# Attention block with a hand-written order: row maxima partly from sums and differences of keys, transposed on VectorE

## The chip, the core and the metric

The kernel runs on one core of one Trainium2 chip. The metric is the device time in microseconds of one execution; lower is better. Five engines work side by side: TensorE (PE, with its weight loads as PEld), VectorE (DVE), ScalarE (ACT), GpSimd (POOL) and SyncE (SP), which issues almost all DMAs. Matmuls write to PSUM, which has eight banks of 128 partitions by 512 float32 values.

## The reference, cut to what matters

```python
h  = x + A(layernorm(x))        # x is 2048 x 512
h2 = h + B(layernorm(h))

def A(x):                       # 32 heads of 16 columns
    q, k, v = split(x @ wqkv)   # each 32 x 2048 x 16
    p = softmax(q @ k.T * 16 ** -0.5)
    return (p @ v) @ wo

def B(x):                       # 688 = half of 1376 columns
    z = gelu(x @ w_in)
    g = w_sp @ layernorm(z[:, 688:]) + b_sp
    return (z[:, :688] * g) @ w_out
```

The change concerns A alone. B and the projection by `wo` follow behind it and stay as they are.

## The kernel before

All values are float32. Products that must be exact to float32 are written as three matmuls of a high and a low part (`mm3`, lines 78 to 81), and `split` (line 68) makes the two parts.

**Prologue** (lines 176 to 291). `load_x` and `ln_T` normalise 16 blocks of 128 rows and turn them with TensorE transposes. `proj_v` makes V, which stays in SBUF whole, in a tile with 17 columns to a head, the last of them ones, so that the product with V also gives the sum of the weights. `proj_qk` makes Q and K in four blocks of 128 rows; their parts go to `q_scr` and `k_scr` in HBM, and `load_q` and `load_k` fetch them again in the layout of attention: 48 rows for a head (high, low and high part of Q against high, high and low of K), one head in partitions 0 to 47, one in 64 to 111, and a second pair of heads behind them along the free axis. While the later blocks are projected, `ahead` already makes row maxima, one `max_unit` at a time.

**Attention** (lines 335 to 428). The 32 heads form 8 groups of four, the queries 4 blocks of 512, the keys 16 blocks of 128: 512 units `(hg, qb, kb)`, and 32 groups `g` of 16 units. For each unit

- `score` (lines 344 to 352) makes, head by head, the transposed scores of 128 keys against 512 queries in a PSUM tile `s` of one bank (three of them), and ScalarE takes the exponential (line 351). Two further rows of K and Q (rows 48 and 49) subtract the maximum of the query within the matmul; they are ones in K and the negated maximum, in two parts, in Q.
- `weigh` (lines 354 to 362) multiplies the exponentials of the unit before by V: four heads, each in 32 columns of the array and 32 partitions of one PSUM bank `pv`, accumulated over 16 units. Each of these float32 matmuls stands in the trace as two instructions.
- behind the last unit of a group `gather` (line 364) copies `pv` to SBUF on ScalarE and sends it out in eight DMAs; `invert` (line 376) takes the reciprocals of the sums some units later.

The maxima are an exact row maximum over all 2048 keys. `max_unit(m)` (lines 143 to 158) makes the plain scores of 128 queries against 512 keys for two heads, side by side in two halves of the array's rows, in a PSUM tile `m` of two banks (two of them), and VectorE takes the maximum over both at once (line 156). There are 32 units to a group `g`, 1024 in all. Behind the last, `max_rows` (lines 160 to 173) negates and joins them on VectorE, turns them on TensorE, splits them on VectorE and writes them to the Q tile of that group in four DMAs from SP. The maxima run ahead of the scores by 46 units and more (line 414).

What sets the order: the kernel's framework builds the queue of each engine itself. It takes the instructions that are ready by its own estimate, in the order of the program where it can, and adds the semaphores. So the order of scores, maxima and products on the engines is not that of the source.

**After attention** (lines 432 to 560) come `make_h`, `make_z`, `gate` and `finish`. The first two blocks of `make_h` and three of `load_o` lie inside the last units of attention (lines 419 to 426).

## Time and profile before

| what | us |
|---|---|
| median of 3 runs | 2244.03 (2243.89 to 2246.54) |
| the profiled execution, its own time | 2244.85 |
| its span, first to last instruction | 2243.1 |
| first score matmul | 189.5 |
| start of the last copy of `pv` to SBUF | 1741.6 |
| granted TensorE clock, mean | 0.996 |

The profile is of one execution. A row of a group of instructions has the line, the engine, the operation, the tiles (out<-in), the shapes, the count, then the busy time in us and the mean of one in ns, then the idle time in front of them and what ended it. A row of the timeline has the start in us, the time in us, then the engine, the line and the tiles; several like instructions in a row are merged, with their count. A row of stages has the stretch, its length, then for each engine the busy time and the count, the granted TensorE clock, the busy share of the DMA engines and their rate.

### The profile page before, as it was taken

How to read it: one execution, taken by the hardware profiler on the slowest of the kernel's cores; microseconds unless marked ns; L12 is line 12 of the kernel's file. 1: busy time of each engine (PE TensorE's matmuls, PEld its weight loads, DVE VectorE, ACT ScalarE, POOL GpSimd, SP SyncE). 2: the span in 40 equal slices, each digit the busy share in tenths (PEclk: the TensorE clock that was granted, in tenths of full speed). 3: DMA queues.
4: the chain of work that ended last, by engine and by line, in shares of the span. 5: the costliest groups of instructions: out<-in, count | busy, mean ns of one | idle time of the engine just before them, and what ended most of it. 6: DMA issues, size and time to landing. Idle time of an engine off the chain costs nothing.

```text
span 2243.1 us, 30649 instructions
## 1 busy us (share of the span) xinstructions
PE 2182.3 (97%) x11824; PEld 1103.7 (49%) x11824; DVE 1554.9 (69%) x1940; ACT 1227.7 (55%) x2333; POOL 101.0 (5%) x76
## 2 busy tenths in 40 slices
PE   8999999999999999999999999999999999999999
PEld 6764333333333333333333333333332899999997
DVE  8477778888888888888888888888851787322222
ACT  2114566777766777767777677776776333111111
POOL 2000020000000000000000000000000222200000
PEclk9999999999999999999999999999999999999999
DMA  5553121110020020011012001100101333423221
GB/s 166 116 150 77 29 72 42 30 31 12 20 30 11 17 42 13 11 30 22 18 21 30 13 11 32 27 11 11 33 5 37 97 121 115 155 100 104 83 72 35
DMA packets 81610, 115.17 MB, mean 51 GB/s; under 512 B 22872, under 2 KB 44392, under 8 KB 77880
## 3 DMA queue, kind: packets, MB, share of 16 engines
q1 hardware_dynamic: 81432, 113.21, 19.4%
q8 instruction: 93, 1.52, 0.3%
q14 instruction: 53, 0.43, 0.1%
q0 software_dynamic: 32, 0.01, 0.0%
HBM read 76.98 MB, written 35.26 MB: 50 GB/s over the span
## 4 chain that ended last, share of the span: by engine, by line
PE 89%; ACT 5%; DMA 2%; DVE 2%; issue 1%; SPq 0%; POOL 0%; ACTq 0%; POOLq 0%; DVEq 0%
PE pv L359 28%; PE s L348 24%; PE m L154 10%; PE acc L79 5%; PE acc L81 5%; PE acc L80 5%; ACT pt L351 4%; PE g L80 4%; PE g L79 4%; PE g L81 4%; DMA xg<-in_x 1%; DMA kst<-k_scr 1%; PE tp L539 0%; ACT o L367 0%; DMA rc<-r_scr 0%
## 5 line engine op out<-in xcount | busy, mean ns | idle before, releaser
L156 DVE TENSOR_REDUCE mx<-m 128x2 f32<-128x1024 f32 x1024 | 1220.6, 1222 | 254.3 <-PE m L154 232.5
L351 ACT ACTIVATE pt<-s 128x512 f32<-128x512 f32 x2048 | 1065.6, 603 | 463.7 <-PE s L348 431.6
L348 PE MATMUL s<-qst,kst 50*128 50x512 f32 x2048 | 701.7, 469 | 42.0 <-ACT pt L351 29.1
L359 PE MATMUL pv<-pt,V 128*32 128x512 f32 x4096 | 695.2, 605 | 0.3 <-ACT o L367 0.3
L348 PEld LDWEIGHTS s<-qst,kst 50*128 50x128 f32 x2048 | 283.1, 184 | 698.9 <-issue 434.5
L154 PE MATMUL m<-kst,qst 48*128 48x512 f32 x2048 | 413.7, 417 | 5.2 <-DVE mx L156 2.9
L154 PEld LDWEIGHTS m<-kst,qst 48*128 48x128 f32 x2048 | 214.1, 185 | 147.5 <-DVE mx L156 131.4
L359 PEld LDWEIGHTS pv<-pt,V 128*32 128x32 f32 x4096 | 112.0, 108 | 172.8 <-issue 172.2
L79 PE MATMUL g<-z,ws 128*128 128x344 f32 x512 | 165.3, 323 | 0.5 <-ACT z L472 0.5
L80 PE MATMUL g<-z,ws 128*128 128x344 f32 x512 | 164.6, 322 | 0.0
L81 PE MATMUL g<-z,ws 128*128 128x344 f32 x512 | 163.4, 319 | 0.0
L71 ACT ACTIVATE ws<-wt 128x1024 fp32r<-128x1024 f32 x32 | 33.6, 1055 | 211.4 <-PE g L80 203.5
L528 DVE SCALAR_TENSOR_TENSOR pr<-g,bias,z 128x344 f32<-128x344 f32 x32 | 18.4, 576 | 182.2 <-PE g L81 180.1
L80 PEld LDWEIGHTS g<-z,ws 128*128 128x128 f32 x512 | 96.1, 188 | 5.8 <-issue 5.2
L79 PEld LDWEIGHTS g<-z,ws 128*128 128x128 f32 x512 | 96.2, 188 | 0.9 <-ACT z L472 0.8
L81 PEld LDWEIGHTS g<-z,ws 128*128 128x128 f32 x512 | 96.2, 188 | 0.6
L315 POOL TENSOR_TENSOR o<-o,rc 128x512 f32<-128x512 f32 x16 | 20.6, 1290 | 1480.6 <-DMA rc<-r_scr 1263.8
L79 PE MATMUL acc<-wi,hT 128*128 128x344 f32 x256 | 83.1, 325 | 0.0
L80 PE MATMUL acc<-wi,hT 128*128 128x344 f32 x256 | 81.8, 319 | 0.0
L81 PE MATMUL acc<-wi,hT 128*128 128x344 f32 x256 | 81.8, 319 | 0.0
L472 ACT ACTIVATE z<-acc 128x344 f32<-128x344 f32 x64 | 29.2, 458 | 82.8 <-PE acc L81 77.4
L71 ACT ACTIVATE part<-acc 128x512 fp32r<-128x512 f32 x32 | 19.1, 597 | 97.3 <-PE acc L81 83.0
(105 smaller groups left out, 1382.5 us busy)
## 6 DMA issues: line engine op xcount, KB each, us to landing
wt<-in_w_sp SPq DMA_DIRECT2D x16, 1024.0 KB
qst<-q_scr SPq DMA_DIRECT2D x192, 64.0 KB
kst<-k_scr SPq DMA_DIRECT2D x48, 256.0 KB
k_scr<-part SPq DMA_DIRECT2D x16, 512.0 KB
q_scr<-part SPq DMA_DIRECT2D x16, 512.0 KB
z_scr<-z SPq DMA_DIRECT2D x16, 344.0 KB
z<-z_scr SPq DMA_DIRECT2D x16, 344.0 KB
xg<-in_x SPq DMA_DIRECT2D x16, 256.0 KB
```

Of the source, the lines that this page charges most:

```text
L71: nc.scalar.activation(hi, src, AF.Copy)
L79: nc.tensor.matmul(ps, lh, rh, start=first, stop=False)
L80: nc.tensor.matmul(ps, lh, rl, start=False, stop=False)
L81: nc.tensor.matmul(ps, ll, rh, start=False, stop=last)
L154: nc.tensor.matmul(t[:, j, :], q[r, p, u * P:(u + 1) * P], k[r, p, c * 512:(c + 1) * 512], start=True, stop=True)
L156: nc.vector.reduce_max(mx[g][:, :, p * 4 + u, c], t, axis=AX.X)
L315: nc.gpsimd.tensor_mul(o, o, rc)
L348: nc.tensor.matmul(s, k[r, h // 2, kb * P:(kb + 1) * P], q[r, h // 2, :], start=True, stop=True)
L351: nc.scalar.activation(t, s, AF.Exp, scale=DH ** -0.5)
L359: nc.tensor.matmul(pv[0][32 * j:32 * j + 32, :], V[:, kb, c:c + 32], pts[j], start=kb == 0, stop=kb == NB - 1)
L472: nc.scalar.activation(zc_, acc[:, :FC], AF.Gelu_apprx_tanh)
L528: nc.vector.scalar_tensor_tensor(pr[:, f], g[i][:, :FC], bias[:, tb:tb + 1], z1[:, f], op0=ALU.add, op1=ALU.mult)
```

## The change

It has these parts.

1. **Order.** `tc.manual_schedule` makes the queues of PE, ACT and DVE (in the prologue SP too) follow the source. The prologue is written out block by block: V, Q and K, the layer norm of two blocks at a time with its last step on ScalarE, and a `take` of each PSUM result one projection later. In attention one round of the loop is two units, and the eight steps of a `max_pair` stand at fixed places among scores and products.
2. **Scores.** A tile `s` has two banks (two tiles instead of three single banks); two heads go into it side by side, and one exponential takes 1024 values to a partition.
3. **Maxima.** A `max_pair` covers 128 queries, two heads (t = 0, 1) and all keys, in eight matmuls of one bank each (three banks, one buffer each). Head t = 1 takes four maxima over 512 keys. For head t = 0 the kernel also keeps the sum and the difference of keys 0 to 511 and 512 to 1023 (`uv`, made in the prologue, through HBM to a tile `uvs`). Since max(a, b) is half of (a + b) + |a - b|, ScalarE takes the absolute value of the scores against the differences, and one VectorE instruction adds the scores against the sums, halves and takes the maximum; two plain maxima cover the other 1024 keys. So VectorE takes seven operands of 512 where it took four of 1024. Maxima run 11 pairs ahead.
4. **Transpose of the maxima.** The negation stays on VectorE, the split goes to POOL, the turning from TensorE to a VectorE transpose of 32 by 32 blocks one round later, and eight DMAs instead of four write the rows.
5. **Accumulator.** `pv` is taken out in halves, one on VectorE, one on ScalarE, and between the product that ends a group and the one that begins the next the order puts other work.
6. **Data.** V goes through HBM (`v_scr`) and comes back for four heads at a time (`load_v`, a POOL copy puts it into place). The heads of a group are numbered by `head`, the rows of Q and K stand interleaved by three, and `load_uv` adds three DMAs for each group of heads.

```diff
-LEAD = 46
-LEAD0 = 40
+LEAD = 11
 KM = 50
+PB = 6
+FIRST = 3
...
-    ps_m = attn.enter_context(tc.tile_pool(name="ps_m", bufs=2, space=PSUM, side="right"))
-    V = vpool.tile([P, NB, H * VW + DH - 1], F32, name="V")
+    ps_m = attn.enter_context(tc.tile_pool(name="ps_m", bufs=1, space=PSUM, side="right"))
+    VP = NB * 4 * VW
+    vst = [vpool.tile([P, VP + DH], F32, name=f"vst{i}") for i in range(2)]
     kst = [kpool.tile([RG + KM, 2, S], F32R, name="kst0")]
-    qst, mx = {}, {}
+    uvs = [kpool.tile([KS, 2, 1024], F32R, name="uvs0")]
...
+    def head(hg, p, t):
+        return 8 * (hg // 2) + 4 * t + 2 * (hg % 2) + p
     def load_k(hg, pieces=range(6)):
-        r = slice(64 * hg, 64 * hg + 64)
         for j in pieces:
             j, t = divmod(j, 2)
-            r0 = RG * t + 16 * j
+            h0 = DH * head(hg, 0, t)
             nc.sync.dma_start(
-                kst[hg % 2][r0:r0 + 16, :, :].bitcast(F32),
-                k_scr[(0, 0, 1)[j], r, :].rearrange("(p t r) s -> t r p s", t=2, r=DH)[t])
+                kst[hg % 2][RG * t + j:RG * t + KS:3, :, :].bitcast(F32),
+                k_scr[(0, 0, 1)[j], h0:h0 + 2 * DH, :].rearrange("(p r) s -> r p s", r=DH))
+    def load_uv(hg, pieces=range(3)):
+        r = slice(32 * (hg % 2), 32 * (hg % 2) + 32)
+        for j in pieces:
+            nc.sync.dma_start(
+                uvs[hg % 2][j:KS:3, :, :].bitcast(F32),
+                uv_scr[(0, 0, 1)[j], hg // 2, r].rearrange("(p r) i s -> r p (i s)", r=DH))
+    def load_v(hg):
+        raw = vpool.tile([P, NB, 4 * DH], F32, name="raw")
+        for t in range(2):
+            c = DH * head(hg, 0, t)
+            nc.sync.dma_start(raw[:, :, 2 * DH * t:2 * DH * t + 2 * DH],
+                              v_scr[:, c:c + 2 * DH].rearrange("(a p) c -> p a c", p=P))
+        nc.gpsimd.tensor_copy(
+            vst[hg % 2][:, :VP].rearrange("p (a c) -> p a c", c=VW)[:, :, :DH],
+            raw.rearrange("p a (h c) -> p (a h) c", c=DH))
...
-    def max_unit(m):
-        g, i = divmod(m, 32)
+                    qst[g][RG * t + j:RG * t + KS:3, :, :].bitcast(F32),
+                    q_scr[(0, 1, 0)[j], h0:h0 + 2 * DH, c].rearrange("(p r) s -> r p s", r=DH))
+    more = {}
+    def bank(i):
+        if i in more:
+            return more[i]()
+        return ps_m.tile([P, 512], F32, name=f"m{i}")
+    def max_pair(m):
+        g, i = divmod(m, 8)
         hg, qb = divmod(g, NQ)
...
+        q, k, w = qst[g], kst[hg % 2], uvs[hg % 2]
         if i == 0:
...
+            mx[g] = sm.tile([P, 16, 4], F32, name="mx")
+            nc.gpsimd.memset(mx[g][:, :8, 3:], LOW)
+        c, p = slice(i % 4 * P, i % 4 * P + P), i // 4
+        at = lambda t, e: mx[g][:, t * 8 + i, e:e + 1]
+        def scores(t, keys, b):
+            r = slice(RG * t, RG * t + KS)
+            acc = bank(b)
+            nc.tensor.matmul(acc, q[r, p, c], keys[r, p], start=True, stop=True)
+            return acc
+        def one(t, e, b):
+            acc = scores(t, k[:, :, 512 * e:512 * e + 512], b)
+            nc.vector.reduce_max(at(t, e if t else e - 1), acc, axis=AX.X)
+        def minus(b):
+            acc = scores(0, w[:, :, 512:], b)
+            ab[0] = sm.tile([P, 512], F32, name="ab")
+            nc.scalar.activation(ab[0], acc, AF.Abs)
+        def plus(b):
+            acc = scores(0, w[:, :, :512], b)
+            nc.vector.tensor_tensor_reduce(ab[0], acc, ab[0], 0.5, LOW, ALU.add, ALU.max, at(0, 0))
+        def last(b):
+            one(0, 3, b)
+            if i == 7:
+                nm = sm.tile([P, 2, 8], F32, name="nm")
+                nc.vector.tensor_reduce(nm.rearrange("p t i -> p (t i)"), mx.pop(g), axis=AX.X,
+                                        op=ALU.max, negate=True)
+                parts = sm.tile([P, 2, 2, 8], F32R, name="mparts")
+                split(parts[:, :, 0], parts[:, :, 1], nm, "pool", "pool")
+                turned[0] = (g, parts)
+        ab = {}
+        four = [lambda b, e=e: one(1, e, b) for e in range(4)]
+        return [four[0], lambda b: one(0, 2, b), minus, four[1], four[2], four[3], plus, last]
+    def max_rows():
+        g, parts = turned.pop(0)
+        t = sm.tile([P, 32], F32, name="mturned")
+        nc.vector.transpose(t, parts.bitcast(F32).rearrange("p t j i -> p (t j i)"))
+        for n in range(P // 32):
+            for j in range(2):
+                r0 = RG * j + KS
+                nc.sync.dma_start(
+                    qst[g][r0:r0 + 2].bitcast(F32).rearrange("r p (c n s) -> r (p c) n s", n=4, s=32)[:, :, n],
+                    t[32 * n + 16 * j:32 * n + 16 * j + 16, :])
...
+                hh = P // 2
+                if which == 1 and n < 2:
+                    kf[n] = p2.tile([P, 512], F32, name=f"kf{n}", bufs=1)
+                    nc.scalar.activation(kf[n][:hh], acc[:hh], AF.Copy)
+                    nc.scalar.activation(kf[n][hh:], acc[:hh], AF.Copy, scale=1.0 - 2.0 * n)
+                if which == 1 and n == 1:
+                    uv = p2.tile([P, 512], F32, name="uv", tag="xn")
+                    nc.gpsimd.tensor_add(uv, kf[0], kf[1])
+                    part = p2.tile([P, 2, 512], F32R, name="part", bufs=PB)
+                    split(part[:, 0, :], part[:, 1, :], uv, "pool", "pool")
+                    for i in range(2):
+                        nc.sync.dma_start(uv_scr[:, b, :, i, :].rearrange("i p s -> p i s"),
+                                          part[hh * i:hh * i + hh].bitcast(F32))
...
+        todo, done = [], [0]
+        def ahead(k):
+            for _ in range(k):
+                m = done[0] // 8
+                if not todo and m < LEAD:
+                    steps = max_pair(m)
+                    todo.extend(steps[i] for i in (0, 1, 3, 2, 4, 6, 5, 7))
+                if todo:
+                    todo.pop(0)(done[0] % 5)
+                    done[0] += 1
...
+            for j in range(24):
+                b, n, i = 1 + j // 8, j // 2 % 4, 1 - j % 2
+                def between(d):
+                    if d == 1 and j >= FIRST:
+                        ahead(5)
+                    if d == 2 and takes:
+                        takes.pop(0)()
+                    if d == 3 and turned and done[0] % 8 > 3:
+                        max_rows()
+                if j in (2, 10):
+                    put = load_wqk(b + 1)
+                if j in (5, 13):
+                    put()
+                if j == 4:
+                    load_v(0)
+                if j in (8, 12):
+                    load_q(j // 4 - 1)
+                if j == 16:
+                    fixed(kst[0])
+                takes.append(proj_qk(b, n, i, between))
+            takes.pop(0)()
+            ahead(8 * LEAD - done[0])
+        m = LEAD
...
-        def score(hg, qb, kb, h):
+        def score(hg, qb, kb, p):
             q, k = qst[hg * NQ + qb], kst[hg % 2]
-            s = ps_s.tile([P, 512], F32, name="s")
-            r = slice(RG * (h % 2), RG * (h % 2) + KM)
-            nc.tensor.matmul(s, k[r, h // 2, kb * P:(kb + 1) * P], q[r, h // 2, :],
-                             start=True, stop=True)
-            t = pp.tile([P, 512], F32, name="pt")
+            s = ps_s.tile([P, 2, 512], F32, name="s")
+            for t in range(2):
+                r = slice(RG * t, RG * t + KM)
+                nc.tensor.matmul(s[:, t, :], k[r, p, kb * P:(kb + 1) * P], q[r, p, :],
+                                 start=True, stop=True)
+            t = pp.tile([P, 2, 512], F32, name="pt")
             nc.scalar.activation(t, s, AF.Exp, scale=DH ** -0.5)
...
-                c = (4 * hg + j) * VW
-                nc.tensor.matmul(pv[0][32 * j:32 * j + 32, :], V[:, kb, c:c + 32],
-                                 pts[j], start=kb == 0, stop=kb == NB - 1)
-            if kb == NB - 1:
-                gather(hg, qb)
-            o = sm.tile([P, 512], F32, name="o", bufs=1)
-            nc.scalar.activation(o, pv[0], AF.Copy)
+            o = pp.tile([P, 512], F32, name="o", bufs=1)
+            nc.vector.tensor_copy(o[:, :256], pv[0][:, :256])
+            nc.scalar.activation(o[:, 256:], pv[0][:, 256:], AF.Copy)
...
-        for n, (hg, qb, kb) in enumerate(units):
-            if hg + 1 < HG and n % 64 < 24 and n % 4 == 1:
-                load_k(hg + 1, [n % 64 // 4])
-            if kb == 1 and n // NB + 3 < HG * NQ:
-                load_q(n // NB + 3)
-            pts = [score(hg, qb, kb, h) for h in range(2)]
-            if prev is not None:
-                weigh(*prev)
-            pts += [score(hg, qb, kb, h) for h in range(2, 4)]
-            prev = (hg, qb, kb, pts)
-            if kb == 5 and n > NB:
-                invert()
-            while m < min(LEAD0 + 9 * (n + 1) // 4, LEAD + 2 * (n + 1), 32 * HG * NQ):
-                max_unit(m)
+        with tc.manual_schedule(engines={E.PE, E.Activation, E.DVE}):
+            for n in range(0, len(units), 2):
+                (hg, qb, kb), (_, _, kb1) = units[n:n + 2]
+                if hg + 1 < HG and n % 64 < 24 and n % 4 == 0:
+                    load_k(hg + 1, [n % 64 // 4])
+                if hg + 1 < HG and n % 64 < 12 and n % 4 == 2:
+                    load_uv(hg + 1, [n % 64 // 4])
+                if hg + 1 < HG and n % 64 == 30:
+                    load_v(hg + 1)
+                if kb == 2 and n // NB + 3 < HG * NQ:
+                    load_q(n // NB + 3)
+                steps = max_pair(m) if m < 8 * HG * NQ else []
                 m += 1
-            if n % 32 == 16 and n < 6 * 32:
-                load_weights(n // 32)
-            if n == 480:
-                load_o(0)
-            if n == 504:
-                make_h(0, ps_m.tile([P, 2, 512], F32, name="m")[:, 0, :])
-                load_o(1)
-            if n == 508:
-                make_h(1, ps_m.tile([P, 2, 512], F32, name="m")[:, 0, :])
-                load_o(2)
-        weigh(*prev)
-        invert()
+                step = lambda b: steps and steps.pop(0)(b)
+                pts = [score(hg, qb, kb, 0), score(hg, qb, kb, 1)]
+                step(2)
+                step(0)
+                if prev is None:
+                    pv[0] = ps_v.tile([P, 512], F32, name="pv")
+                    for j in range(4):
+                        nc.tensor.matmul(pv[0][32 * j:32 * j + 32, :], vst[0][:, :32],
+                                         vst[0][:, :512], start=True, stop=True)
+                else:
+                    weigh(*prev)
+                step(1)
+                if kb == 0 and n:
+                    gather(*units[n - 1][:2])
+                step(2)
+                pts1 = [score(hg, qb, kb1, 0)]
+                step(0)
+                pts1.append(score(hg, qb, kb1, 1))
+                step(1)
+                step(2)
+                weigh(hg, qb, kb, pts)
+                if turned:
+                    max_rows()
+                step(1)
+                prev = (hg, qb, kb1, pts1)
+                if kb == 6 and n > NB:
+                    invert()
+                if n % 32 == 16 and n < 6 * 32:
+                    load_weights(n // 32)
+                if n == 480:
+                    load_o(0)
+                if n == 504:
+                    make_h(0, bank(0))
+                    load_o(1)
+                if n == 508:
+                    make_h(1, bank(0))
+                    load_o(2)
+            weigh(*prev)
+            gather(*prev[:2])
+            invert()
     attn.close()
```

256 lines of the change are left out of this document (148 added, 108 removed).

## The prediction

> **What bounds the kernel now.** I read the page first, then a table of stages, then the steady part of attention instruction by instruction.
>
> ```profile
> span 2243.1 us, 30649 instructions
> ...
> PE 2182.3 (97%) x11824; PEld 1103.7 (49%) x11824; DVE 1554.9 (69%) x1940; ACT 1227.7 (55%) x2333; POOL 101.0 (5%) x76
> ...
> PE 89%; ACT 5%; DMA 2%; DVE 2%; issue 1%; SPq 0%; POOL 0%; ACTq 0%; POOLq 0%; DVEq 0%
> ```
>
> ```profile
> 0.00:189.50 189.50, 177.17 (x743) 124.16 (x743) 130.40 (x286) 36.64 (x61) 18.88 (x22) 0.96 0.54 142
> 189.50:1742.00 1552.50, 1509.71 (x8169) 520.92 (x8169) 1207.23 (x1134) 1082.89 (x2083) 31.06 (x17) 1.00 0.12 25
> 1742.00:2243.00 501.00, 495.37 (x2912) 458.61 (x2912) 217.26 (x521) 108.16 (x190) 51.05 (x37) 1.00 0.30 98
> ```
>
> PE is called busy everywhere, but the end of a matmul is modelled, so the share says little. The stages (prologue, attention, rest) say where to look: attention takes 1552 of 2243 us, and in it neither DVE (1207) nor ACT (1083) is full. So I look at one unit; the timelines of PE, of DVE and of ACT in the same stretch:
>
> ```profile
> 751.26 1.11 PE L359 MATMUL pv<-pt,V 128*32 128x512 f32 x8
> 752.29 0.50 PE L348 MATMUL s<-qst,kst 50*128 50x512 f32 x2
> 752.63 0.65 PE L154 MATMUL m<-kst,qst 48*128 48x512 f32 x4
> 753.11 0.91 PE L348 MATMUL s<-qst,kst 50*128 50x512 f32 x2
> 753.95 1.11 PE L359 MATMUL pv<-pt,V 128*32 128x512 f32 x8
> 755.00 0.50 PE L348 MATMUL s<-qst,kst 50*128 50x512 f32 x2
> ```
>
> ```profile
> 753.06 2.36 DVE L156 TENSOR_REDUCE mx<-m 128x2 f32<-128x1024 f32 x2 [0.35 <-PE m L154]
> ```
>
> ```profile
> 752.88 2.06 ACT L351 ACTIVATE pt<-s 128x512 f32<-128x512 f32 x4 [0.64 <-PE s L348]
> ```
>
> ```profile
> 753.53 0.18 PEld L348 LDWEIGHTS s<-qst,kst 50*128 50x128 f32 x1 [0.47 <-ACT pt L351]
> ```
>
> A unit takes 752.29 to 755.00, 2.71 us. It is a circle: ACT waits 0.64 us for the first score; the fourth score waits for the end of the first exponential, because `s` has three banks; `pv` stands behind the fourth score; the next unit's first score stands behind `pv`. No engine is full; the order and the banks make the 2.71. Between units stands one disturbance in each group of 16:
>
> ```profile
> L163 DVE TENSOR_REDUCE nm<-mx x20: 219/220/222, 663.6 to 1562.5; 128x16 f32<-128x64 f32 x20
> ```
>
> ```profile
> 900.19 1.04 PE L359 MATMUL pv<-pt,V 128*32 128x512 f32 x2
> ...
> 901.17 0.28 PE L166 MATMUL m<-ident,nm 128*16 128x128 f32 x1
> ...
> 901.48 0.28 DVE L75 CAST mpart<-m 16x128 fp32r<-16x128 f32 x1 [1.27 <-PE m L166]
> ...
> 902.03 1.06 PE L359 MATMUL pv<-pt,V 128*32 128x512 f32 x6
> ```
>
> A group takes (1562.5 - 663.6) / 19 = 47.31 us, 16 x 2.71 is 43.4, so `max_rows` costs 3.9: DVE waits for the turning, and the four heads of `pv` fall apart into two and six instructions, each part at the 1.04 us of all eight. Two units cost 47.31 / 8 = 5.91.
>
> **The change part by part.** First the prices, from the groups by shape.
>
> ```profile
> L156 DVE TENSOR_REDUCE mx<-m 128x2 f32<-128x1024 f32 x1024 | 1220.6, 1222 | 254.3 <-PE m L154 232.5 <-PE s L348 20.5
> L351 ACT ACTIVATE pt<-s 128x512 f32<-128x512 f32 x2048 | 1065.6, 603 | 463.7 <-PE s L348 431.6 <-PE m L154 31.6
> ...
> L71 ACT ACTIVATE ws<-wt 128x1024 fp32r<-128x1024 f32 x32 | 33.6, 1055 | 211.4 <-PE g L80 203.5 <-DMA wt<-in_w_sp 7.2 <-PE acc L80 0.7
> ...
> L76 DVE TENSOR_TENSOR part<-acc,part 128x512 fp32r<-128x512 f32 x32 | 21.9, 685 | 14.4 <-ACT part L71 14.3
> ...
> L239 DVE COPY V<-acc 128x512 f32<-128x512 f32 x16 | 11.0, 688 | 7.9 <-PE acc L81 7.8
> ...
> L71 ACT ACTIVATE o<-o 128x512 fp32r<-128x512 f32 x16 | 10.1, 630 | 9.0 <-PE acc L80 5.5 <-issue 2.0 <-POOL o L315 1.5
> ```
>
> ```profile
> 85.02 0.39 PE L80 MATMUL acc<-xT,wqk 128*128 128x512 f32 x1
> 85.24 0.39 PE L81 MATMUL acc<-xT,wqk 128*128 128x512 f32 x1
> ```
>
> *DVE, 512 from PSUM:* 0.69 (copy and two-operand row); two reductions back to back take 2.36, not 2.44, so 0.08 overlaps: 0.61. *ACT:* four exponentials in 2.06, so (2.06 - 0.60) / 3 = 0.49 each; 1024 instead of 512 adds 1.055 - 0.630 = 0.43, so 0.92 each, 1.03 alone. *PE:* a matmul 0.23; the first behind `pv` 0.34 (752.29 to 752.63); the one before `pv` 0.42 (753.53 to 753.95); `pv` itself 1.04; matmuls in the two halves of the rows side by side at no price, as the s x2 and m x4 rows show.
>
> *One round (two units) in the new order, PE.* First half: `last` 0.34, two score pairs 0.23 each, the maxima matmuls `four0` and `one2` side by side 0.42, `pv` 1.04: 2.26. Second half: `minus` with `four1` 0.34, score pair 0.23, `four2` beside one head of the next pair 0.23, its other head 0.23, `four3` with `plus` 0.42, `pv` 1.04: 2.49. Sum 4.75, if nothing waits.
>
> *The waits that the single banks add.* `plus` needs the bank of `four1`: matmul 0.50 (the duration of the first row behind `pv`), about 0.05 to the reader, reduction 0.69, 0.05 back: 1.29 behind the start of the half, where PE alone would be there after 1.03. `four3` needs the bank of `minus`, which ScalarE empties: 0.59 (752.29 to 752.88), 0.60, 0.05: 1.24. So 0.26 more: **5.01 a round** against 5.91. Queued behind these waits on PE are `pv`, `last` and the next scores; on ACT the absolute value stands ahead of the exponentials three and four, which are wanted only a round later.
>
> *Do the others keep up?* ACT: 4 x 0.92 + 0.49 = 4.17, and the next round's second score needs the fourth exponential's bank: the third starts at about 3.3 (behind the absolute value, 2.26 + 0.59 + 0.49), the fourth ends at 3.3 + 0.92 + 1.03 = 5.25, wanted at 5.01 + 0.57. It fits. DVE: 7 x 0.61 = 4.3 to 7 x 0.69 = 4.8, with the work of a group's end (negation 0.22, transpose, half copy and reciprocal, each between that and 0.69, so about 1.1 in eight rounds) 4.4 to 5.0. It just fits. The new instruction that adds, halves and takes the maximum is in no row: from below 0.69 (L76 reads the same two operands), from above 1.22 (as if it read them one after the other, L156). I take 0.69, since L76 is the nearest row.
>
> *Transpose of the maxima:* the 3.9 of each group go. On PE nothing is left of it. The split on POOL has 3 us until the transpose; POOL is busy 31 us in all of attention. SP issues eight DMAs:
>
> ```profile
> 901.79 2.83 SPq L172 DMA_DIRECT2D qst<-mpart  x4
> ```
>
> 8 x 0.71 = 5.7 and the landing, for which I take 2 to 4. From the transpose (late in the round with kb 10) to the first score of the next group are three rounds less 4.6, so 10.4 us. It fits with 1 to 3 us to spare.
>
> *Accumulator in halves:* the product behind it finds its bank empty; ACT's half (between 0.28 and 0.60) pushes exponentials three and four, for which 0.3 is to spare. I allow 0.3 for each of 31 group ends: 9.
>
> *Prologue.* Before, 40 `max_unit`s stand between projection matmuls:
>
> ```profile
> 117.63 0.40 PE L81 MATMUL acc<-xT,wqk 128*128 128x512 f32 x1
> 117.96 0.49 PE L154 MATMUL m<-kst,qst 48*128 48x512 f32 x2
> 118.38 0.50 PE L79 MATMUL acc<-xT,wqk 128*128 128x512 f32 x1
> 118.72 0.39 PE L80 MATMUL acc<-xT,wqk 128*128 128x512 f32 x1
> ```
>
> One costs 1.09 - 2 x 0.23 = 0.63, 40 of them 25. After, 88 matmuls come in 18 batches of five, three slots each: 0.63 + 2 x 0.23 = 1.09, 20 in all. The same 576 projection matmuls stay. So the first score comes at 189.5 - 25 + 20 = 184, if the waits stay as they are. DVE has 0.61 x 4.4 + 0.69 = 3.4 for each projection of 2.7 + 1.1, so it does not hold PE. V through HBM, `uv` and their DMAs hide behind 0.54 DMA share; `load_v(0)` has 19 projections until its use. K has to be there before the first maxima:
>
> ```profile
> 107.21 0.70 PE L154 MATMUL m<-kst,qst 48*128 48x512 f32 x2 [1.18 <-DMA kst<-k_scr]
> ```
>
> Before, PE waited for it; now six projections (16 us) stand between, and SP, whose order is fixed here too, holds V's writes behind `load_k`'s wait, for which the six buffers are cover. Without the cover some 5 us.
>
> *Tail.* From round 245 on no maxima are left: ACT sets the pace, 4 x 0.92 = 3.7, eleven rounds 40. The two `make_h` inside stand in PE's fixed order with 12 matmuls, 3.3 each: 7. ACT and DVE now wait in order for the data of `load_o(0)`: 0 to 10, I take 3.
>
> **The sum.** 184 + 245 x 5.01 (1227) + 9 + 40 + 7 + 3 = 1470 at the last copy of `pv`, where it was 1741.6; the rest, 2243.1 - 1741.6 = 501.5, is untouched: span 1971.5, and the 1.75 us that the execution (2244.85) has beyond its span: **1973**. The profiled execution lies 0.04% above the median of the runs, so nothing is to be scaled.
>
> **The rivals.**
>
> *PE without waits.* If the banks come free in time (shorter matmul-to-reader times than the 0.55), a round is 4.75: 245 x 0.26 = 64 less, 1909. For it: PE is the fullest engine. Against: the 0.50 and the 0.59 are rows.
>
> *VectorE becomes the bound.* Seven reductions of 512 where there were four of 1024: none overlaps its neighbour, since each now waits for its own matmul, and the new instruction costs 1.22: 6 x 0.69 + 1.22 + 0.14 = 5.5 a round, 245 x 0.49 = 120 more, 2093; with half of that, 2033. The Trainium skill speaks for this one: its page "VectorE: DVE Perf Modes", section "Rules for kernel authors", asks for few instructions, as each ends with a flush of the pipeline that a missing semaphore doesn't save. By that rule the count decides, and it goes from four to seven; the trace agrees that 0.16 of the 0.69 is not streaming (1.22 - 0.69 = 0.53 is what 512 more cost).
>
> *The maxima come late.* If a DMA of the rows costs twice 0.71 in queue and landing, 13.4 are needed where 10.4 are to be had: 3 at each of 31 group ends, 93 more, 2066.
>
> *The order does not hold what it says:* the group ends keep their 3.9 (from another wait, such as ACT's or DVE's head of the queue on `load_o`, `sums` or the accumulator): 31 x 3.9 = 121 more, 2094.
>
> *Slower.* The new VectorE instruction streams at a quarter of the pace: 4 x 0.53 + 0.16 = 2.3. DVE then needs 6 x 0.69 + 2.3 + 0.14 = 6.6 a round, 245 x 1.6 = 390 more, 2363. It decides from about 6.1 a round, (1741.6 - 184 - 59) / 245, that is from 1.8 for this instruction, 2.7 times the row of L76. For it speaks only that the trace has no such instruction.
>
> **How the numbers follow.** Forecast 1973: 0.50, from 1940 to 2010 by the bounds of prologue, `load_o` and group ends. PE without waits 0.15, VectorE 0.14, late maxima 0.08, order 0.07, slower 0.04; 0.02 for no change by some of these together. The range goes from 1890 (the first rival with a K that no longer waits) to 2085, which takes in late maxima and most of VectorE's. Faster 0.94, same (within 0.2%, 4.5 us, about what a measurement of this kernel can tell) 0.02, slower 0.04.
>
> **What would show it.** In the profile after: rounds of 5.0 us between the starts of every second `pv`, with `four3`/`plus` waiting about 0.3 for ACT or DVE; groups at 40 us by the `nm` rows; the first score at 184; DVE at nine tenths in attention; the new instruction at 0.69. If DVE is full and PE waits for it in front of `four0`, the VectorE rival holds; if scores wait for DMAs of the `mturned` rows, the maxima are late.

## The result, and the profile after

The changed kernel takes 1943.5 us (median of four runs, 1942.1 to 1945.3), the kernel before 2244.0 in the same session: a ratio of 0.866, with a 95% interval of 0.8645 to 0.8675. Forecast were 1973 us and a range of 1890 to 2085. One run of those below, of the kernel before in a fixed order, came at a lower clock than the other three and 1.9% above the fastest of them; its ratio leaves it out.

The page of the changed kernel, its first lines and the head of its chain of work:

```profile
span 1943.5 us, 32016 instructions
...
PE 1916.7 (99%) x11800; PEld 1096.1 (56%) x11800; DVE 1443.8 (74%) x2916; ACT 1266.8 (65%) x1591; POOL 139.2 (7%) x200
...
PE 92%; DVE 2%; ACT 2%; issue 1%; DMA 1%; SPq 0%; POOL 0%; ACTq 0%; DVEq 0%
```

The table of stages, cut at the first score and at the last copy out of `pv` (span; then busy time of PE, PEld, DVE, ACT and POOL with their counts, granted clock, DMA share, GB/s):

```profile
0.00:184.50 184.50, 170.03 (x745) 125.25 (x745) 118.78 (x283) 59.34 (x98) 36.08 (x49) 0.98 0.69 181
184.50:1441.00 1256.50, 1251.04 (x8144) 512.53 (x8144) 1109.55 (x2112) 1100.01 (x1304) 50.49 (x113) 0.99 0.15 36
1441.00:1943.00 502.00, 495.61 (x2914) 458.28 (x2912) 215.41 (x521) 107.43 (x190) 52.62 (x38) 1.00 0.30 100
```

The prologue is 5 us shorter, attention 296 us shorter, and the rest as long as it was. In the prologue TensorE is busy for 170.0 us where it was 177.2, 7.1 less where 5 less were forecast, and idle for 14.5 where it was 12.3. In attention VectorE now has work for 1110 of 1257 us, ScalarE for 1100.

The groups, by the negation of the maxima that each group has once (the view of one line, in the steady stretch from 700 to 1300 us):

```profile
L217 DVE TENSOR_REDUCE nm<-mx x15: 220/220/221, 718.8 to 1265.3; 128x16 f32<-128x64 f32 x15
```

That is (1265.3 - 718.8) / 14 = 39.04 us a group, or 4.88 a round, where it was 47.31 and 5.91. One round in the timeline of TensorE, and the stretch of VectorE and ScalarE that belongs to its second half:

```profile
800.50 0.50 PE L197 MATMUL m<-kst,qst 48*128 48x512 f32 x1
800.50 0.96 PE L537 MATMUL s<-qst,kst 50*128 50x512 f32 x4
801.24 0.45 PE L197 MATMUL m<-kst,qst 48*128 48x512 f32 x2
801.62 1.07 PE L548 MATMUL pv<-pt,vst 128*32 128x512 f32 x8
802.62 0.49 PE L197 MATMUL m<-uvs,qst 48*128 48x512 f32 x1
802.62 0.50 PE L197 MATMUL m<-kst,qst 48*128 48x512 f32 x1
802.95 0.40 PE L537 MATMUL s<-qst,kst 50*128 50x512 f32 x2
803.20 0.39 PE L197 MATMUL m<-kst,qst 48*128 48x512 f32 x1
803.33 0.50 PE L537 MATMUL s<-qst,kst 50*128 50x512 f32 x2
803.82 0.50 PE L197 MATMUL m<-kst,qst 48*128 48x512 f32 x1
803.93 0.49 PE L197 MATMUL m<-uvs,qst 48*128 48x512 f32 x1
804.35 1.06 PE L548 MATMUL pv<-pt,vst 128*32 128x512 f32 x8
805.34 0.49 PE L197 MATMUL m<-kst,qst 48*128 48x512 f32 x1
```

```profile
803.18 1.89 DVE L202 TENSOR_REDUCE mx<-m 128x1 f32<-128x512 f32 x3 [0.23 <-PE m L197]
804.99 0.68 DVE L211 CUSTOM_DVE_ANT_0 ab<-m,ab 128x512 f32<-128x512 f32 x1
```

```profile
803.16 0.60 ACT L207 ACTIVATE ab<-m 128x512 f32<-128x512 f32 x1
```

The round takes 4.84 us, 800.50 to 805.34; over the 600 us of steady attention the starts of every second `pv` lie 4.87 apart in the median. The first half goes from 800.50 to 802.62, 2.12 us without a wait. The second takes 2.72: behind `minus` and `four1` (802.62) and the scores stands `four3` (803.82), which needs the bank that ScalarE's absolute value left at 803.16 + 0.60, and then `plus` (803.93), which needs the bank of the reduction that began at 803.18. The product `pv` starts only behind them. These are the two waits that the prediction named. Over 600 us of attention they are the two waits for a bank that count; the table of waits (us in total, times, longest; a weight load that waits beside a running matmul is counted too, and 278 waits in 123 rounds are more than those of `plus`, so the sums are larger than what the round loses):

```profile
PEld m L197 <- DVE mx L202: 213.5, 278, 0.8
...
PEld m L197 <- ACT ab L207: 38.6, 123, 0.4
```

One group is not like the others: group 30 begins late, and the copies out of `pv` around its start stand 44.5 us apart instead of 39.0. TensorE and SP's queue there:

```profile
1356.62 0.49 PE L197 MATMUL m<-kst,qst 48*128 48x512 f32 x1
1359.88 1.85 PE L537 MATMUL s<-qst,kst 50*128 50x512 f32 x4 [2.77 <-DMA qst<-mturned]
```

```profile
1343.45 9.71 SPq L497 DMA_DIRECT2D rc<-r_scr  x10
1353.27 6.05 SPq L235 DMA_DIRECT2D qst<-mturned  x8
```

SP's order is left to the planner in attention, and it put the small DMAs of the first `load_o` ahead of the eight DMAs that carry the maxima. The scores waited 2.77 us for those, and the group lost about as much again behind the wait (44.5 - 39.0 - 2.8 = 2.7): the granted clock in the next ten microseconds is 0.50 (last but two of the columns).

```profile
1360.00:1370.00 10.00, 10.00 (x38) 4.13 (x38) 5.31 (x10) 5.58 (x8) 0.00 (x0) 0.50 0.06 12
```

### The profile page after: what moved, and what is told of

Same layout as the page of the kernel before. It is cut to its first block, busy times and chain, and to the rows that moved or that the text cites. A ratio compares the mean times of both kernels' runs of the same rounds, so it can differ in the third digit from the quotient of the medians.

```text
span 1943.5 us, 32016 instructions
## 1 busy us (share of the span) xinstructions
PE 1916.7 (99%) x11800; PEld 1096.1 (56%) x11800; DVE 1443.8 (74%) x2916; ACT 1266.8 (65%) x1591; POOL 139.2 (7%) x200
## 4 chain that ended last, share of the span: by engine, by line
PE 92%; DVE 2%; ACT 2%; issue 1%; DMA 1%; SPq 0%; POOL 0%; ACTq 0%; DVEq 0%
PE pv L548 25%; PE m L197 25%; PE s L537 13%; PE acc L84 6%; PE acc L85 5%; PE acc L86 5%; PE g L85 4%; PE g L84 4%; PE g L86 4%; ACT pt L540 1%; PE tp L754 1%; DMA rc<-r_scr 0%; PE tp L671 0%; DVE rs_t L99 0%; PE tp L197 0%
## 5 line engine op out<-in xcount | busy, mean ns | idle before, releaser
L540 ACT ACTIVATE pt<-s 128x1024 f32<-128x1024 f32 x1024 | 994.1, 1029 | 148.1 <-PE s L537 140.2
L202 DVE TENSOR_REDUCE mx<-m 128x1 f32<-128x512 f32 x1511 | 958.4, 683 | 112.9 <-PE m L197 70.9
L197 PE MATMUL m<-kst,qst 48*128 48x512 f32 x1511 | 609.8, 449 | 0.0
L548 PE MATMUL pv<-pt,vst 128*32 128x512 f32 x4096 | 547.5, 606 | 0.0
L537 PE MATMUL s<-qst,kst 50*128 50x512 f32 x2048 | 472.6, 431 | 6.9 <-DMA qst<-mturned 2.8
L197 PE MATMUL m<-uvs,qst 48*128 48x512 f32 x503 | 250.0, 498 | 0.0
L197 PEld LDWEIGHTS m<-uvs,qst 48*128 48x128 f32 x503 | 92.1, 183 | 208.8 <-DVE mx L202 206.1
L211 DVE CUSTOM_DVE_ANT_0 ab<-m,ab 128x512 f32<-128x512 f32 x252 | 171.2, 679 | 3.7 <-ACT ab L207 2.0
L207 ACT ACTIVATE ab<-m 128x512 f32<-128x512 f32 x251 | 151.0, 602 | 18.6 <-PE tp L197 10.4
L84 PE MATMUL acc<-wi,hT 128*128 128x344 f32 x256 | 83.1, 325 | 0.0
L85 PE MATMUL acc<-wi,hT 128*128 128x344 f32 x256 | 81.8, 319 | 0.0
```

The source lines that it names most:

```text
L84: nc.tensor.matmul(ps, lh, rh, start=first, stop=False)
L85: nc.tensor.matmul(ps, lh, rl, start=False, stop=False)
L197: nc.tensor.matmul(acc, q[r, p, c], keys[r, p], start=True, stop=True)
L202: nc.vector.reduce_max(at(t, e if t else e - 1), acc, axis=AX.X)
L207: nc.scalar.activation(ab[0], acc, AF.Abs)
L211: nc.vector.tensor_tensor_reduce(ab[0], acc, ab[0], 0.5, LOW, ALU.add, ALU.max, at(0, 0))
```

## The experiments

The theory at this point: a round is TensorE's own time plus the wait of `plus` and `four3`, and the fixed order is what keeps the round and frees the group ends of their 3.9 us. That the place of the turn of the maxima decides the group ends became the theory only after the fourth run. Rivals were that VectorE's work sets the round, that the order alone does it, and, later, that it is the turn's engine or the shape of the scores. Each kernel is told by its edit; groups are read as above, from the rows of `nm` between 700 and 1300 us.

**Four plain maxima for each head.** Head t=0 takes its maxima like head t=1, without sums, differences and absolute value:

```diff
-            nc.vector.reduce_max(at(t, e if t else e - 1), acc, axis=AX.X)
+            nc.vector.reduce_max(at(t, e), acc, axis=AX.X)
...
-        return [four[0], lambda b: one(0, 2, b), minus, four[1], four[2], four[3], plus, last]
+        return [four[0], lambda b: one(0, 2, b), lambda b: one(0, 0, b), four[1], four[2],
+                four[3], lambda b: one(0, 1, b), last]
```

> The changed kernel, but head t = 0 takes four plain maxima over 512 keys like head t = 1: no sums and differences in the maxima, no absolute value on ScalarE; order and all else kept. Theory (the round is PE's order plus the wait for the banks of the second half): the bank of the third-last matmul now comes free by a second VectorE reduction, 1.90 us behind the start of the half instead of 1.29, so a round goes from 4.85 to about 5.45, a group of 16 units from 39.0 to about 43.7, the whole to about 2090 us. Rival (VectorE's work alone counts: eight times 0.61 instead of seven): 4.85 to 5.1, about 2000 us. Rival (the order is the whole gain): no change, 1943 us.

Measured 2082.7 us, ratio 0.928 (0.926 to 0.930). The rows of `nm`, and VectorE's timeline in one round:

```profile
L216 DVE TENSOR_REDUCE nm<-mx x13: 220/220/221, 740.3 to 1265.6; 128x16 f32<-128x64 f32 x13
```

```profile
812.92 3.08 DVE L201 TENSOR_REDUCE mx<-m 128x1 f32<-128x512 f32 x5 [0.24 <-PE m L196]
```

Groups take 43.8 us: five reductions follow each other in the second half, 3.08 us, and TensorE waits for them. So the sums and differences are worth 139 us here, 4.7 a group, close to what the theory said: with them, one of the five banks of the second half goes to ScalarE, which reads it beside VectorE.

**Two matmuls less, VectorE's work kept.** `minus` and `plus` are left out with ScalarE's absolute value (so head t=0's maxima are incomplete); VectorE reduces 512 constants in SBUF in the place of `plus`:

```diff
+    still = const.tile([P, 512], F32, name="still")
+    nc.gpsimd.memset(still, LOW)
...
-        return [four[0], lambda b: one(0, 2, b), minus, four[1], four[2], four[3], plus, last]
+        none = lambda b: None
+        kept = lambda b: nc.vector.reduce_max(at(0, 0), still, axis=AX.X)
+        return [four[0], lambda b: one(0, 2, b), none, four[1], four[2], four[3], kept, last]
```

> The changed kernel without the matmuls minus and plus and without the absolute value; VectorE instead takes a maximum over 512 constants in SBUF at the place of plus, so it keeps seven instructions of 512 a round. It leaves out keys 0 to 1023 from the maximum of head t = 0. Theory (the wait for the banks of the second half sets the round, not VectorE's work): no bank is used twice in the second half, the round falls to what PE needs, 2.12 + 2.36 = 4.5 us, a group to about 36, the whole to about 1860 us. Rival (VectorE is the bound): round stays at 4.8 to 4.85, 1940 us.

Measured 1878.2 us, ratio 0.837 (0.836 to 0.838). The rows of `nm`, and the 600 us of steady attention in a table of stages:

```profile
L219 DVE TENSOR_REDUCE nm<-mx x16: 220/220/221, 726.4 to 1283.1; 128x16 f32<-128x64 f32 x16
```

```profile
700.00:1300.00 600.00, 593.04 (x3870) 234.27 (x3870) 575.07 (x968) 504.80 (x532) 13.09 (x52) 1.00 0.13 28
```

Groups of 37.1, 4.64 a round. So the two matmuls, their banks and ScalarE's absolute value, which went out together, carry 65 us of the 1943: the rival's 1940 us is ruled out, and the theory's 1860 us and groups of 36 are missed by 18 us and 1.1 us. With 575 of 600 us VectorE is nearly full here, and in its table of waits those of the maxima matmuls for VectorE are the longest in total for TensorE (242.5 us in 315 waits), so the floor is not TensorE's alone. The VectorE rival was wrong for the changed kernel and becomes right about 5% below it.

**The changed kernel without the fixed order in attention.** The prologue keeps it:

```diff
-        with tc.manual_schedule(engines={E.PE, E.Activation, E.DVE}):
+        with ExitStack():
             for n in range(0, len(units), 2):
```

> The changed kernel with the fixed order taken away in attention alone: PE, ACT and DVE are queued by the framework's planner there; the prologue keeps its order. Theory (the order is needed for the round of 4.85): the four heads of pv fall apart again and the maxima are pulled between the scores, a group takes 43 to 48 us instead of 39.0, the whole 2070 to 2230 us. Rival (the shorter work of VectorE, the wide exponentials and the transpose on VectorE make the gain whatever the order): a group 39 to 40, 1945 to 1975 us.

Measured 2044.5 us, ratio 0.911 (0.909 to 0.912), between the two forecasts: the first is wrong about the steady groups, the rival about the ends. Its rows of `nm`, and two stages, cut at the copies out of `pv` of its first and its fourth group:

```profile
L217 DVE TENSOR_REDUCE nm<-mx x15: 219/220/222, 723.7 to 1270.3; 128x16 f32<-128x64 f32 x15
```

```profile
242.70:428.00 185.30, 176.08 (x778) 62.30 (x777) 109.11 (x206) 109.64 (x127) 27.02 (x22) 0.85 0.18 48
428.00:1420.00 992.00, 990.71 (x6496) 408.64 (x6496) 908.09 (x1725) 874.54 (x1041) 18.26 (x82) 1.00 0.13 30
```

The steady groups take 39.04, as in the fixed order: the planner finds the same round. It loses at the start, where three groups take 185 us in place of 117 with a clock of 0.85, starts attention at 195.1 instead of 184.5, and takes 133 us for the last three groups in place of 120. There the first forecast's mechanism does act: the planner pulls the maxima ahead, and from 241.6 to 281 us TensorE runs 48 maxima matmuls beside 12 of the scores. In attention the fixed order is worth 101 us, and all of it at the ends; in the prologue it was not tried.

**The kernel before in a fixed order.** TensorE, ScalarE and VectorE are held to the source order in its attention:

```diff
-        for n, (hg, qb, kb) in enumerate(units):
+        with tc.manual_schedule(engines={E.PE, E.Activation, E.DVE}):
+            for n, (hg, qb, kb) in enumerate(units):
...
```

> The kernel before, with PE, ACT and DVE held to the order of the source in attention, nothing else: scores of two heads, pv of the unit before, scores of the other two, two maxima. Theory (order alone isn't enough: with three single banks the second score of a unit waits for the third exponential of the unit before, 1.24 + 0.42 + 1.0 us behind each other): 2.66 a unit where it was 2.71, a group 43 to 45 us because the group ends and the ends of attention get shorter, the whole 2100 to 2150 us. Rival (order is the whole gain): a unit 2.4, a group 39 to 40.5, 1970 to 2010 us.

Measured 2274.7 us (median of four, 2262.7 to 2304.7), ratio 1.012 (1.0075 to 1.016): some 26 us slower, and both forecasts missed. TensorE's timeline at a group end, and the stretch behind it:

```profile
884.81 0.27 PE L166 MATMUL m<-ident,nm 128*16 128x128 f32 x1 [2.55 <-DVE nm L163]
```

```profile
886.20:896.40 10.20, 10.20 (x44) 4.55 (x40) 5.11 (x5) 5.53 (x11) 0.00 (x0) 0.51 0.01 3
```

The turn is asked for right behind the last maxima, and in a fixed order TensorE stands before it until VectorE has reduced and negated: 2.55 us. After that the granted clock is halved, here for 10.2 us, and behind the last turn for 68 us. Units at full clock take 2.71 as they did; a group takes 48.05. So the order alone does not shorten this kernel, and with the turn at this place the group ends cost more in a fixed order than under the planner; the place of the turn was next to be tried.

**The changed kernel again,** with no edit, beside the next three kernels on one chip, as the measure for small differences:

> The changed kernel unchanged, on the same chip as the other three, as the measure for differences of a few us: 1942 to 1946 us by every theory.

Measured 1943.2 us, ratio 0.866 (0.864 to 0.867).

**The changed kernel with its maxima turned by TensorE.** The transpose goes back to TensorE and bank 0, with VectorE's split from PSUM and four DMAs, at the changed kernel's place:

```diff
-        t = sm.tile([P, 32], F32, name="mturned")
-        nc.vector.transpose(t, parts.bitcast(F32).rearrange("p t j i -> p (t j i)"))
+        t = bank(0)
+        nc.tensor.transpose(t[:16, :P], nm.rearrange("p t i -> p (t i)"), ident)
+        part = sm.tile([16, 2, P], F32R, name="mpart")
+        split(part[:, 0, :], part[:, 1, :], t[:16, :P])
...
```

> The changed kernel, with one part taken back: the row maxima are turned by TensorE into bank 0 and split by VectorE from PSUM, with four DMAs in place of eight; the order and all else stay as changed. Theory (a turn in TensorE is cheap once its place is fixed and its input is there long before; the 3.9 us of each group were a wait in an order that asked for the maxima too soon): TensorE pays the turn of 0.28 and two changes of kind of matmul, VectorE two small instructions of 0.28 and a wait, together 0.5 to 1.2 us for each of 29 groups in attention: groups 39.5 to 40.2, 1958 to 1978 us. Rival (the turn in TensorE is itself what cost the 3.9): groups 43, 2055 to 2070 us.

Measured 1946.4 us, ratio 0.867 (0.866 to 0.868) against 1943.2 unchanged. Its rows of `nm`, and TensorE behind the product:

```profile
L217 DVE TENSOR_REDUCE nm<-mx x15: 219/220/222, 722.1 to 1273.0; 128x16 f32<-128x64 f32 x15
```

```profile
764.97 0.28 PE L229 MATMUL m<-ident,nm 128*16 128x128 f32 x1
765.17 0.50 PE L197 MATMUL m<-kst,qst 48*128 48x512 f32 x1
```

A turn in TensorE costs 0.20 us there and no wait, and a group 39.35: 0.3 more, less than the theory's lower end. Four DMAs take 3.13 us of SP's queue at group 30 where eight took 6.05, and the late start of that group does not happen, which gives 5 us back: 29 x 0.3 - 5 is about the 3 us measured. That is what the transpose on VectorE is worth together with POOL's split and its eight DMAs, and the two intervals overlap.

**The accumulator taken out whole.**

```diff
-            nc.vector.tensor_copy(o[:, :256], pv[0][:, :256])
-            nc.scalar.activation(o[:, 256:], pv[0][:, 256:], AF.Copy)
+            nc.scalar.activation(o, pv[0], AF.Copy)
```

> The changed kernel, with the accumulator taken out whole by ScalarE (one copy of 128x512) at the same place. Theory (the next product of weights and V stands a whole half round behind the copy, and 0.60 instead of about 0.35 us of ScalarE fits into its idle share): 0 to 0.2 us for each of 31 group ends, 1943 to 1950 us. Rival (ScalarE's first exponential of the next half comes late and PE waits for its bank): 0.6 us or more for each group end, 1962 us or more.

Measured 1949.4 us (1944.3 to 1957.6), ratio 0.867 (0.866 to 0.868), against 1943.2 unchanged. The intervals overlap; steady groups are 0.2 us longer, at the upper end of the theory, and 29 of them make 6 us, as much as the medians differ. The profiled execution is the slowest of the five; group 30 is late in it too (45.3 us where the unchanged kernel's takes 44.5 and 44.8), and why its runs scatter by 13 us is open. The halves are worth some 6 us, not clear of the scatter.

**The rows of the maxima first.** SP is held to the source order too, and `load_o` is cut in two:

```diff
-        with tc.manual_schedule(engines={E.PE, E.Activation, E.DVE}):
+        with tc.manual_schedule(engines={E.PE, E.Activation, E.DVE, E.SP}):
...
-                if n == 480:
-                    load_o(0)
+                if n in (480, 492, 500):
+                    load_o((480, 492, 500).index(n))
+                if n == 498:
+                    split_o(0)
```

> The changed kernel, with SP's queue held to the source order in attention too, so that the twelve small DMAs of the first load_o are issued behind the eight DMAs of the row maxima of group 30, and with load_o cut in two: its DMAs and GpSimd's product at units 480, 492 and 500, its split by ScalarE and VectorE at 498, 504 and 508. Theory (the one late group end, 44.5 us where the others take 39.0, comes from those DMAs alone): group 30 starts without the wait, 5 us less, 1936 to 1940 us, ratio to the kernel before 0.863 to 0.865. Rival (SP in source order queues other DMAs behind one that waits): as much lost elsewhere, 1943 to 1965 us.

Measured 1937.3 us (1936.1 to 1942.1), ratio 0.863 (0.862 to 0.864). SP's timeline:

```profile
1345.93 5.33 SPq L235 DMA_DIRECT2D qst<-mturned  x8
```

The eight DMAs go out right behind the transpose, group 30 starts without a wait, and the time is 6 us less, as the theory said; the interval just touches that of the unchanged kernel. This is the fastest of the versions here that compute everything.

**Scores in three banks.** The scores go back to tiles of 128x512 with one exponential each, in three banks:

```diff
-        ps_s = at.enter_context(tc.tile_pool(name="ps_s", bufs=2, space=PSUM))
+        ps_s = at.enter_context(tc.tile_pool(name="ps_s", bufs=3, space=PSUM))
...
-            s = ps_s.tile([P, 2, 512], F32, name="s")
+            w = pp.tile([P, 2, 512], F32, name="pt")
             for t in range(2):
+                s = ps_s.tile([P, 512], F32, name="s")
...
-            nc.scalar.activation(t, s, AF.Exp, scale=DH ** -0.5)
...
+                nc.scalar.activation(w[:, t, :], s, AF.Exp, scale=DH ** -0.5)
...
```

> The changed kernel with its scores in three banks of 128x512 as before the change, one exponential of 512 for each score, and all else as changed (the bank that becomes free stays unused). Theory (the fourth score of a unit waits for the first exponential when there are three banks, 1.24 us behind the first score, and the product of weights and V stands behind it; in the second half ScalarE's absolute value stands ahead of that exponential): first half 2.8, second half 3.0 to 3.4, a round 5.8 to 6.2, 2170 to 2290 us. Rival (the rounds got shorter by the order and by pairing maxima matmuls, and a third or a fourth bank makes no difference): 1940 to 1970 us.

Measured 2358.2 us, ratio 1.053 (1.047 to 1.059). Its rows of `nm`, TensorE's two waits in a round, and its 600 us of steady attention:

```profile
L217 DVE TENSOR_REDUCE nm<-mx x12: 219/220/221, 733.2 to 1299.1; 128x16 f32<-128x64 f32 x12
```

```profile
800.91 0.49 PE L538 MATMUL s<-qst,kst 50*128 50x512 f32 x1 [0.70 <-ACT pt L540]
...
803.97 0.50 PE L538 MATMUL s<-qst,kst 50*128 50x512 f32 x1 [0.45 <-ACT pt L540]
```

```profile
700.00:1300.00 600.00, 488.65 (x2987) 175.00 (x2989) 433.94 (x794) 434.37 (x852) 8.68 (x39) 1.00 0.11 25
```

Groups of 51.4: the fourth score of each half waits for the first exponential, as in the kernel before, and `pv` and the maxima stand behind it. The theory held in kind, but a round takes 6.43 us, above its 6.2, and the whole 68 us more than its upper end: TensorE, VectorE and ScalarE now wait by turns, with 489, 434 and 434 of 600 us busy.

**Scores in four single banks.** The same with four; the edit stands against the kernel with three:

```diff
-        ps_s = at.enter_context(tc.tile_pool(name="ps_s", bufs=3, space=PSUM))
+        ps_s = at.enter_context(tc.tile_pool(name="ps_s", bufs=4, space=PSUM))
```

> The changed kernel with its scores in four banks of 128x512 and one exponential of 512 for each score in place of two banks pairs and exponentials of 1024. Theory (what counts is the fourth bank; eight exponentials at 0.49 and an absolute value at 0.49 are 4.4 us of a round of 4.85): 4.85 to 5.0 a round, 1943 to 1985 us. Rival (the wide exponentials are what makes ScalarE fast enough): rounds of 5.2 or more, 2030 us or more.

Measured 1949.0 us, ratio 0.8685 (0.867 to 0.870).

```profile
L217 DVE TENSOR_REDUCE nm<-mx x15: 220/220/221, 721.1 to 1270.0; 128x16 f32<-128x64 f32 x15
```

Groups of 39.2. Against three banks the fourth gives 409 us; the wide exponentials give some 6, with overlapping intervals. With three banks the changed kernel is slower than the kernel before (2358.2 against 2244.7).

**The kernel before, fixed order, with a later turn.** As the kernel before in a fixed order, but TensorE's turn is asked for two units behind the negation:

```diff
+        turned.append([2, g, nm])
...
+                if turned:
+                    turned[0][0] -= 1
+                    if turned[0][0] < 0:
+                        turn_rows()
...
```

> The kernel before with TensorE, ScalarE and VectorE held to the source order in attention (as in the run that came out at 2275 us), and the turn of the row maxima by TensorE asked two units behind the negation of the maxima instead of right behind it. Theory (in source order TensorE waited 2.5 us for the negated maxima in each group, and that wait is what a group end costs): groups of 43.4 + 0.5 to 1.2, 28 of them 3 to 4 us shorter than in that run, 2150 to 2200 us. Rival (the turn in TensorE between the maxima matmuls, or its bank, costs the time, wherever it stands): groups of 47 and more, 2250 to 2290 us.

Measured 2125.5 us, ratio 0.948 (0.945 to 0.951).

```profile
800.97 0.28 PE L173 MATMUL m<-ident,nm 128*16 128x128 f32 x1 [1.06 <-DVE mx L156]
```

```profile
L163 DVE TENSOR_REDUCE nm<-mx x14: 219/220/222, 708.0 to 1284.9; 128x16 f32<-128x64 f32 x14
```

Groups of 44.4, a group end of 1.0 (44.4 - 16 x 2.71) where the fixed order had 4.7; what is left is 1.06 us for a bank. The turn still runs on TensorE. Forecast were 2150 to 2200, missed by 25: 28 groups of 3.7 less are 103 us, and the 68 us of half clock behind the last turn, which were not allowed for, are gone too.

**The same later turn under the planner.** The order is left as it was in the kernel before.

> The kernel before, its order left to the planner, with the turn of the row maxima asked two units behind the negation of the maxima. Theory (the 3.9 us of a group end come from a turn that is asked at once, with products of weights and V and VectorE's split stuck around it): groups of 43.9 to 44.6, 28 x 3 less, 2145 to 2175 us. Rival (the planner puts the turn where it did, or the group end costs the same wherever it stands): 2235 to 2250 us.

Measured 2167.7 us, ratio 0.966 (0.964 to 0.967).

```profile
L163 DVE TENSOR_REDUCE nm<-mx x13: 219/220/221, 731.9 to 1268.6; 128x16 f32<-128x64 f32 x13
```

Groups of 44.7, just above the theory's 44.6, and a time within its range: the place of the turn is worth 77 us to the old kernel without any other part of the change.

## Why the prediction was right, and where its terms were off

These steps held: two different halves, two waits for banks in the second, nothing left of the 3.9 us at a group end, the same rest. The reason given for the third did not. The sum came out 28 us above the profiled execution of the changed kernel (1945.3 us, 1.8 of them outside the span). The parts, in us:

```
                                              forecast   measured
until the first score                          184.0      184.5
245 rounds, group ends, wait for load_o(0)    1239.0     1204.0
eleven rounds without maxima, two make_h        47.0       52.7
from the last copy out of pv to the end        501.5      502.3
outside the span                                 1.75       1.8
```

The cuts are the first and last copies out of `pv` and, for the 246th round, its first score in TensorE's timeline:

```profile
L555 ACT ACTIVATE o<-pv x32: 378/402/403, 227.8 to 1441.2; 128x256 f32<-128x256 f32 x32
```

```profile
1388.52 0.96 PE L537 MATMUL s<-qst,kst 50*128 50x512 f32 x4
```

*The round* is the term that was mis-sized: 5.01 forecast, 4.84 in the round shown (800.50 to 805.34) and 4.87 in the median. The second half was right, 2.72 for 2.75: `plus` 1.31 behind its start (forecast 1.29), 0.42 to `pv`, 0.99 for `pv`. The first half was 2.26 in the forecast and is 2.12: the four scores beside `last` take 0.74 to the next maxima matmul (0.80), the pair before `pv` 0.38 (0.42, which had been read from a matmul that had just waited), and `pv` 1.00 (1.04). 0.14 in 245 rounds is 34 us, more than the whole difference; the tail and `load_o` below took part of it back.

*Group ends:* 39.04 - 8 x 4.87 is 0.1 a group; 0.3 was allowed.

*The 3.9 us of a group.* They went, as forecast, but the step gave them to the turn by TensorE, and that was not it; this term is right in part by luck, since the same edit also moved the turn to a later place. Turned by TensorE at the changed kernel's place, a group is 0.3 longer; and the old kernel with TensorE's turn two units later has group ends of 1.0 in a fixed order and 1.4 under the planner. So the place decides. How it costs differs. In a fixed order TensorE waits 2.55 us for the negated maxima, and the clock falls behind that. Under the planner, in the kernel before, the input was there: the negation ends at 900.21, and the turn began at 901.17.

```profile
899.99 0.22 DVE L163 TENSOR_REDUCE nm<-mx 128x16 f32<-128x64 f32 x1
```

```profile
898.49 1.11 PE L359 MATMUL pv<-pt,V 128*32 128x512 f32 x8
...
916.24 1.10 PE L359 MATMUL pv<-pt,V 128*32 128x512 f32 x8
```

There VectorE waits 1.27 us for the turn, and the order stays disturbed behind it: five units take 17.75 us, 4.2 more than 5 x 2.71, and `pv` falls into two and six instructions in three of them. With the later turn under the planner it does so in one, and VectorE no longer waits for the turn. How much of the 3.9 us was VectorE's wait and how much the order behind it, no run separates.

*load_o:* 3 us were allowed for ScalarE and VectorE at the head of their queues. It cost 5.5, by SP's queue: the maxima came late in one of 31 group ends, as in the rival at 2066, though by other DMAs ahead in the queue and not by the price of the eight, and the clock fell behind it. That rival's price of 3 us for each was right for the wait (2.77); it happened once.

*Tail:* ScalarE sets the pace there, as forecast, with 4.02 a round, not 3.7. Four exponentials of 1024 one behind the other in ScalarE's timeline:

```profile
1415.59 3.87 ACT L540 ACTIVATE pt<-s 128x1024 f32<-128x1024 f32 x4 [0.15 <-PE s L537]
```

The pitch is (3.87 - 1.03) / 3 = 0.95 where 0.92 had been worked out, and 0.15 is waited in each round besides.

*VectorE* was to have 4.4 to 5.0 a round and has 1110 / 1257 of 4.88, 4.3. A page of the Trainium skill spoke for the rival that it becomes the bound ("VectorE: DVE Perf Modes", section "Rules for kernel authors": the number of operations is what to keep small). The trace does not show that price here: three reductions of 512 take 1.89, so the second and third cost (1.89 - 0.68) / 2 = 0.60 each; in the kernel before the second of two reductions of 1024 cost 2.36 - 1.22 = 1.14, or 0.57 for each 512. Twice the count costs 0.03 for each 512 where reductions follow each other, some 0.2 a round. The kernel with VectorE's work kept shows where the rival begins, at rounds of 4.64.

*The rivals.* TensorE without waits, 1909: the waits are there. The order that does not hold: it holds. The slow new instruction: 0.68 was measured for 0.69.

What each part is worth depends on the others, and the values do not add up to the 300 us. Taken out of the changed kernel alone: the fourth bank of scores 409 us (three single banks against four), the sums and differences 139, the fixed order in attention 101, the halves of the accumulator some 6, the transpose on VectorE some 3. Put into the old kernel alone: a fixed order loses some 26, a later turn gains 77, both together 119. Not tried: the order of the prologue alone, and the old kernel with four banks of scores, for which it has no PSUM beside its pairs of maxima banks.

## What to carry to other kernels

Where an engine's instructions stand in order, look for the instruction whose input is computed just before it, and move it a few steps later before moving it to another engine: here the place was worth 77 us under the planner and some 143 in a fixed order, the engine some 3. Count banks against the latency from matmul to reader and back (1.20 to 1.31 us in the round shown): a bank more or less decided over 409 us, while wider instructions on the same banks gave some 6. A planner may find the same steady round as an order written by hand and still lose at the start and the end, so compare the ends first; and fix the DMA queue's order as well, when something small and late stands in it.

## What the runs showed of the hardware

*A short wait of TensorE can cost its clock.* In the kernel before with a fixed order, 31 group ends leave TensorE idle for 2.4 to 2.6 us, and behind 29 of these the granted clock is halved within three microseconds, for 3.4 to 13.7 us in 28 cases and for 68 behind the last. In the changed kernel the one wait of 2.77 is followed by 10.2 us of half clock, and its group is 5.5 us longer. Waits of 1.06 in each group, in the old kernel with a later turn, never did it. The Trainium skill's page "TensorE: Matmul & The Clock Gate", section "HAM oscillation — how this bites in real kernels", has the bound for such gaps at about 3.4 us; these waits are shorter. No other bound comes out of the runs: the 1.46 us ahead of the first score are followed by 3.4 us of half clock in the changed kernel and by none in the one that turns its maxima on TensorE, and in the run under the planner the clock is halved from 246 to 281 us with no wait over 0.9 us ahead of it.

*The new VectorE instruction* (add, halve and maximum of 512 from PSUM and SBUF) costs as much as a plain reduction of 512, plus a small one that reads its accumulator:

```profile
800.14 0.68 DVE L211 CUSTOM_DVE_ANT_0 ab<-m,ab 128x512 f32<-128x512 f32 x1
800.74 0.08 DVE L211 DVE_READ_ACCUMULATOR2_ANT mx<- 128x1 f32 x1
```
